# Joint products for half blocks of maxima, six weight chunks decoded later, and three smaller moves in a fused attention and two-layer network

## The chip, the core and the metric

The kernel runs on one core of a Trainium2 chip. The core has five engines with a queue of instructions each, which run in order and wait for each other by semaphores: PE (TensorE, matrix products), DVE (VectorE), ACT (ScalarE), POOL (GpSimd) and SP (SyncE, which here issues nearly all DMA transfers). The metric is the device time of one execution in microseconds (us), lower is better.

## What is computed

```python
q_pool = q.reshape(B, H, S // 2, 2, D).mean(axis=3)      # B, H, S, D = 4, 8, 1152, 64
scores = matmul(q_pool, k.transpose(0, 1, 3, 2)) / sqrt(D)
attn = exp(scores - max(scores)); attn = attn / (sum(attn) + 1e-9)
x = matmul(attn, v)                # heads side by side: 2304 tokens x 512
h = x @ moe_w_in;  x = (h * cos(h)) @ moe_w_out          # 512 -> 2048 -> 512
h = x @ moe2_w_in; out = where(h > 0, h, exp(min(h, 0)) - 1) @ moe2_w_out
```

The weights come as 64-bit floats, everything else as 32-bit floats.

## The kernel before

PE multiplies in a fast 32-bit form (fp32r) that keeps fewer bits, so operands are split into a high and a low part and a product becomes two or three products that add up in PSUM. The 64-bit weights are decoded on the chip from their raw words: `decode_tasks` (L84 to L130) gives ten tasks for one half (w_in or w_out) of one of the 16 chunks of a layer: a fetch of 512 KB (`raw`, two buffers), five DVE instructions, an ACT copy to the high part, one more DVE instruction, and two (`far`, L128 and L129) that make the low part, on POOL for the first layer and on DVE for the second. Their work tiles `m` and `e` have two buffers in the attention and one in the MLP (`dec2`, L655).

**Attention.** The 32 heads are worked on in 16 pairs. A pair takes 36 steps, 18 a head (two halves of 288 pooled queries by nine chunks of 128 keys). A step has two products for scores (`ps`, L453 and L455, of which the second takes the row maxima off), an exponential on ACT (`e`, L458), for five chunks of nine a split of `e` into `eh` and `el` (ACT L466, POOL L467), and seven steps later the products with v into `acc` (L482 to L486). Between these the next pair is prepared by a plan of step numbers (L574 to L621): keys and queries are transposed on PE (L340), copied as high parts (L349, L353), low parts are taken (L357, L364), and DMAs place them (L329). The maxima come from `unit` (L394): products of a block of 128 queries with 384 keys into `pm` (L400) and a reduction by DVE (L407). A head has 4.5 blocks of queries, so the fifth block of a pair holds half a block of each head, and its `unit` has two products that add up, each with zeros where the other head's queries stand. Sums of squares (`square`, ACT, L314; five a pair) go to `judge`, whose result `fits` says at the end whether a second, exact network has to run. `weight_work` decodes the first layer's weights meanwhile, paced by step counts (L635); four chunks stay in SBUF, twelve go to DRAM (`w_d`, L150) and are fetched again by `fetch_w` (L154).

The first pair is prepared before the steps begin (L537 to L562): all transposes of both heads, their high and low parts, v, three blocks of maxima of the first head, the sums of squares.

**MLP.** `mlp` runs two layers of six blocks of 384 tokens, each block 16 steps, one chunk of 128 hidden units a step. Step i issues `h_step(i)` (12 products, L673 to L675, then ACT L682 and DVE L683), `g_step(i-1)` (ACT L696 and L697, DVE L699, ACT L704, POOL L705, which make `gh` and `gl`) and `o_step(i-3)` (12 products into `po`, L729; nine wider ones in the second layer). `split_x` (L190) makes the next block's tokens ready in steps 8 to 11: a product with the reciprocal sums (DVE L194, first layer only), the high part (ACT L197), the low part (DVE L198). From the second block on `weight_work(1, ...)` decodes the second layer's weights, four or five tasks a step. `ps_h` has four buffers, so PE can be three steps ahead of `g_step`.

## Time and profile before

| | |
|---|---|
| time, median of 3 runs (lowest to highest) | 1386.76 us (1385.75 to 1387.06) |
| time of the profiled execution | 1385.99 us |
| its span | 1384.2 us |
| PE busy | 1349.6 us, 98% of the span |
| DVE, ACT, POOL busy | 822.8, 819.8, 700.5 us (59%, 59%, 51%) |
| DMA | 177 MB moved, q1 takes 44.9% of 16 engines' span |

The span runs from the first to the last instruction of the program. Products are pipelined: their durations overlap, and what a product takes of PE's time is the distance from its start to the next one's. The table's PE time is the union of overlapping durations. The attention ends and the MLP begins at 567.7 us; the first layer ends at about 970.5 us.

### The profile page before, as it was taken

The page shows a single profiled execution, that of the slowest core. Times are in us where ns is not written, and L with a number is a line of the kernel's source. Part 1 is how long each engine was busy: PE and PEld are TensorE (multiplying, and loading weights), DVE is VectorE, ACT ScalarE, POOL GpSimd, SP SyncE. Part 2 cuts the span into 40 slices and gives each one's busy share as a digit, 9 for nine tenths or more (in the row PEclk, how much of TensorE's full clock was granted, in tenths as well). Part 3 has the DMA queues.
Part 4 walks back from the last instruction along what each step waited for, and adds up shares of the span by engine and source line. Part 5 has one row for each costly group of instructions (what it writes and reads, how often), then busy time and mean ns, then how long its engine had stood idle before and what let it go on. Part 6 is the DMA issues. An engine that isn't in the chain of part 4 may idle for free.

```text
span 1384.2 us, 22762 instructions
## 1 busy us (share of the span) xinstructions
PE 1349.6 (98%) x7683; PEld 1235.9 (89%) x7683; DVE 822.8 (59%) x1454; ACT 819.8 (59%) x2080; POOL 700.5 (51%) x823
## 2 busy tenths in 40 slices
PE   6999999999999999999999999999999999999998
PEld 5888888888888888899999999999999999999997
DVE  5678897887888878236887888788121212111111
ACT  5778878878888787655554555455533433343332
POOL 5668888787888888322232223232333333333332
PEclk9999999999999999999999999999999999999999
DMA  4566667787768775572352535269501010101000
GB/s 97 132 144 148 159 137 188 173 203 179 186 174 198 181 191 137 185 274 96 117 168 93 176 107 189 71 207 364 211 1 47 0 46 1 46 1 46 1 24 26
DMA packets 164543, 177.25 MB, mean 128 GB/s; under 512 B 83872, under 2 KB 135840, under 8 KB 164416
## 3 DMA queue, kind: packets, MB, share of 16 engines
q1 hardware_dynamic: 164416, 175.70, 44.9%
q8 instruction: 63, 1.03, 0.3%
q14 instruction: 64, 0.52, 0.1%
HBM read 105.46 MB, written 43.66 MB: 108 GB/s over the span
## 4 chain that ended last, share of the span: by engine, by line
PE 66%; issue 17%; DVE 8%; POOL 7%; ACT 1%; DMA 0%; POOLq 0%; SPq 0%; DVEq 0%; ACTq 0%
PE po L729 18%; PE acc L486 7%; POOL gl L705 6%; PE ph L675 6%; PE ph L673 6%; PE ph L674 6%; PE pm L400 5%; PE ps L453 5%; PE ps L455 4%; DVE mm L407 3%; PE acc L484 2%; PE acc L482 2%; PE acc L483 2%; PE pk L340 1%; DVE m L117 1%
## 5 line engine op out<-in xcount | busy, mean ns | idle before, releaser
L705 POOL TENSOR_TENSOR gl<-u,gh 128x384 fp32r<-128x384 f32 x192 | 207.6, 1081 | 328.8 <-ACT gh L704 322.5
L467 POOL TENSOR_TENSOR el<-e,eh 128x288 fp32r<-128x288 f32 x320 | 271.8, 857 | 115.7 <-ACT eh L466 83.9
L458 ACT ACTIVATE e<-ps 128x288 f32<-128x288 f32 x576 | 234.4, 413 | 110.1 <-PE ps L455 84.0
L675 PE MATMUL ph<-xh,w 128*128 128x384 f32 x768 | 257.9, 336 | 0.0
L673 PE MATMUL ph<-xh,w 128*128 128x384 f32 x768 | 257.7, 336 | 0.0
L674 PE MATMUL ph<-xl,w 128*128 128x384 f32 x768 | 257.4, 335 | 0.0
L407 DVE TENSOR_REDUCE mm<-pm 128x1 f32<-128x384 f32 x432 | 222.9, 549 | 53.7 <-PE pm L400 52.1
L729 PE MATMUL po<-gh,w 128*128 128x384 f32 x768 | 211.4, 336 | 0.4 <-ACT gh L704 0.4
L453 PE MATMUL ps<-qst,kst 128*128 128x288 f32 x576 | 201.3, 349 | 2.5 <-ACT e L458 2.4
L702 DVE SCALAR_TENSOR_TENSOR u<-ph,a 128x384 f32<-128x384 f32 x96 | 52.8, 554 | 225.7 <-POOL a L688 225.7
L729 PE MATMUL po<-w,gh 128*128 128x512 f32 x576 | 179.6, 393 | 0.0
L400 PE MATMUL pm<-kst,qst 128*128 128x384 f32 x480 | 168.8, 405 | 7.7 <-DVE mm L407 6.1
L686 ACT ACTIVATE a<-ph 128x384 f32<-128x384 f32 x96 | 47.2, 492 | 214.2 <-PE ph L675 210.8
L455 PE MATMUL ps<-q,k 69*128 69x288 f32 x576 | 171.9, 298 | 0.9 <-DVE q L429 0.8
L486 PE MATMUL acc<-e,vt 128*66 128x288 f32 x512 | 166.0, 405 | 0.0
L704 ACT CAST gh<-u 128x384 fp32r<-128x384 f32 x192 | 97.5, 508 | 113.7 <-DVE u L699 88.6
L688 POOL TENSOR_SCALAR a<-a 128x384 f32<-128x384 f32 x96 | 50.3, 524 | 223.6 <-ACT a L687 214.6
L673 PEld LDWEIGHTS ph<-xh,w 128*128 128x128 f32 x768 | 144.3, 188 | 4.1
L674 PEld LDWEIGHTS ph<-xl,w 128*128 128x128 f32 x768 | 144.2, 188 | 3.9
L675 PEld LDWEIGHTS ph<-xh,w 128*128 128x128 f32 x768 | 144.2, 188 | 0.0
L729 PEld LDWEIGHTS po<-gh,w 128*128 128x128 f32 x768 | 140.1, 188 | 1.4 <-ACT gh L704 1.0
L466 ACT CAST eh<-e 128x288 fp32r<-128x288 f32 x320 | 137.0, 428 | 0.0
(87 smaller groups left out, 2548.6 us busy)
## 6 DMA issues: line engine op xcount, KB each, us to landing
w_d<-wd SPq DMA_DIRECT2D x56, 512.0 KB
w<-w_d SPq DMA_DIRECT2D x56, 512.0 KB
raw<-in_moe_w_in_dram SPq DMA_DIRECT2D x32, 512.0 KB
raw<-in_moe_w_out_dram SPq DMA_DIRECT2D x32, 512.0 KB
vt<-in_v_dram SPq DMA_DIRECT2D x32, 288.0 KB
kr<-in_k_dram SPq DMA_DIRECT2D x30, 288.0 KB
k<-uk SPq DMA_DIRECT2D x30, 288.0 KB
qr<-in_q_dram SPq DMA_DIRECT2D x32, 256.0 KB
```

What stands on the lines that cost most here:

```text
L400: nc.tensor.matmul(ps[:, 0:W], qst[:, i * P:(i + 1) * P], kst[:, u * W:(u + 1) * W], start=first, stop=last and not exact)
L407: nc.vector.reduce_max(mm[:, x, u:u + 1], ps[:, 0:W], axis=AX.X)
L453: nc.tensor.matmul(ps[:, 0:HALF], kst[:, c * P:(c + 1) * P], qst[:, qs], start=True, stop=False)
L455: nc.tensor.matmul(ps[:, 0:HALF], k2[0:KR, c * P:(c + 1) * P], q2[0:KR, qs], start=False, stop=True)
L458: nc.scalar.activation(e, ps[:, 0:HALF], AF.Exp, scale=SCALE)
L467: nc.gpsimd.tensor_tensor(el, e, eh.bitcast(F32), ALU.subtract)
L486: nc.tensor.matmul(acc[0:VW, 0:HALF], vt[:, j * NC + c, :], *e, start=first, stop=last)
L673: nc.tensor.matmul(h, wh, xh, start=(c == 0), stop=False)
L674: nc.tensor.matmul(h, wh, xl, start=False, stop=False)
L675: nc.tensor.matmul(h, wl, xh, start=False, stop=(c == KD - 1))
L705: nc.gpsimd.tensor_tensor(gl, u, gh.bitcast(F32), ALU.subtract)
L729: nc.tensor.matmul(o, a, b_, start=st and t == 0, stop=sp and t == 2)
```

## The change

Five things are changed.

1. From the second pair on, the fifth block's `unit` makes one product where it made two: `qd`, a new tile that holds the half blocks of both heads in its two diagonal quarters (copied there by POOL, two copies of 64 x 64 a pair), by the high part of both heads' keys (`uk`). The limit in `judge` is halved.
2. The w_out halves of chunks 4, 6, 8, 10, 12 and 14 of the first layer (`LATE`) are decoded no more during the attention, stored and fetched, but by `late_work` in the first block of the MLP, five tasks a step from step 0 on, straight into the weight tile.
3. The sums of squares of a pair are three instructions, not five: keys in two pieces, all queries in one.
4. The first pair is prepared head by head: queries are loaded from ACT's queue and added on DVE; the first head's transposes, high parts and three blocks of maxima go first (with the high parts of 64 rows alone), then the second head's, for which the transposes are made a second time. The splits of v for the next pair stand at steps 27 and 31 instead of both at 27.
5. In the first layer, from the third block of tokens on, `split_x` runs its two DVE instructions on POOL.

```diff
@@ network
+    LATE = range(NPREW, KF, 2)
@@ weight_work
             for half in range(2):
+                if half and layer == 0 and f in LATE:
+                    continue
...
+    def late_work(dec_p):
+        rest = []
+        for f in LATE:
+            first, *others = decode_tasks(0, f, 1, wt[0, f][:, 1], dec_p)
+            yield first
+            yield from rest
+            rest = others
+        yield from rest
@@ fetch_w
-        for half in range(2):
+        for half in range(1 if layer == 0 and f in LATE else 2):
@@ split_x
+        eng = nc.vector if layer or blk < 2 else nc.gpsimd
         if layer == 0:
-            nc.vector.tensor_tensor(src, src, rb[:, c, :], ALU.mult)
+            eng.tensor_tensor(src, src, rb[:, c, :], ALU.mult)
...
-        nc.vector.tensor_tensor(lo, src, hi.bitcast(F32), ALU.subtract)
+        eng.tensor_tensor(lo, src, hi.bitcast(F32), ALU.subtract)
@@ load
+            queue = nc.sync if n else nc.scalar
             for j in range(2):
-                nc.sync.dma_start(
+                queue.dma_start(
...
-            for c in range(0, NC, step):
-                for j in range(2):
+            for j, c in itertools.product(range(2), range(0, NC, step)):
@@ prep_tasks
-            nfull, tail, third = SQ // P, SQ % P, NC // 3
-            pieces = [(kr[:, third * i:third * (i + 1)], P, i) for i in range(3)] + [(qp[:, 0:nfull], P, 3)]
-            if tail:
-                pieces.append((qp[0:tail, nfull:], tail, 4))
+            nfull, tail = SQ // P, SQ % P
+            pieces = [(kr[:, 0:NC // 2], 0), (kr[:, NC // 2:], 1), (qp, 3)]
...
-                nc.gpsimd.tensor_tensor(
-                    qp[0:m, i0:i1], qr[0:m, i0:i1, :, 0], qr[0:m, i0:i1, :, 1], ALU.add)
+                (nc.gpsimd if n else nc.vector).tensor_tensor(
+                    qp[0:m, i0:i1, js], qr[0:m, i0:i1, js, 0], qr[0:m, i0:i1, js, 1], ALU.add)
...
+                        if n and tag == "q" and blocks[0] == (0 if j else NQB - 2):
+                            src = qst[j][0:D, j * OFF:P] if j else qst[j][0:D, (NQB - 1) * P:SQ]
+                            nc.gpsimd.tensor_scalar(
+                                qd[j * D:(j + 1) * D, j * OFF:j * OFF + SQ % P], src.bitcast(F32),
+                                1.0, 0.0, ALU.mult, ALU.add)
@@ unit
+                if len(parts) == 2 and n and not exact:
+                    nc.tensor.matmul(ps[:, 0:W], qd, highs[n][:, u * W:(u + 1) * W],
+                                     start=True, stop=True)
+                    parts = []
+                kr = slice(0, D) if pool is ps_s and not exact else slice(0, P)
...
-                        ps[:, 0:W], qst[:, i * P:(i + 1) * P], kst[:, u * W:(u + 1) * W],
+                        ps[:, 0:W], qst[kr, i * P:(i + 1) * P], kst[kr, u * W:(u + 1) * W],
@@ judge
-                    fits, both[:, 0:1], (LIMIT * 2.0 ** 12) ** 2 * D, None, ALU.is_le)
+                    fits, both[:, 0:1], (LIMIT * 2.0 ** 11) ** 2 * D, None, ALU.is_le)
@@ attention, before the pairs
+        adds[0]()
+        q_groups[0][0](ps_a, "a", slice(0, 1))
+        for g in k_groups:
+            g[0](heads=slice(0, 1))
+        first = [q_groups[0]] + k_groups
+        for _, high, _ in first:
+            high((0,))
...
+        for t in units(0, HB, ps_s, "s"):
+            t()
...
+        combine(0, 0, HB)
+        spread(0, 0, HB, ps_s, "s")
...
+        for t in adds[1:]:
+            t()
...
+        for put, high, low in q_groups[1:]:
             put(ps_a, "a")
...
+        for put, high, low in first:
+            put(*((ps_a, "a") if low is first[0][2] else ()))
+            high((1,))
+            low((1,))
         split_v(0)
@@ attention, the pairs
-        n_ww = 2 * KF * 10 + (KF - NPREW)
+        n_ww = (2 * KF - len(LATE)) * 10 + (2 * (KF - NPREW) - len(LATE))
...
-                at(SV, lambda: split_v(n + 1))
+                for j in range(2):
+                    at(SV + 4 * j, lambda j=j: split_v(n + 1, (j,)))
@@ mlp
+        late = late_work(dec_p)
...
                 fetch_w(0, NPREW + 4 + i, wp2)
+            if i < KF:
+                run_some(late, 5)
```

PE, pair 1's preparation in the steps of pair 0. First before, then now: `pm_4` is the half-block product, `ps` and `acc` are the steps of the running pair.

```order
L484 MATMUL acc_1_536<-el_17_548,vh_132 66x288
L400 MATMUL pm_3_0_645<-kst_0_279,qst_130 128x384
L400 MATMUL pm_4_0_648<-kst_0_279,qst_130 128x384
L400 MATMUL pm_4_0_648<-kst_1_280,qst_131 128x384
L453 MATMUL ps_7_652<-qst_129,kst_1_166 128x288
L455 MATMUL ps_7_652<-q_1_168,k_1_125 128x288
```

```order
L515 MATMUL acc_1_553<-el_17_565,vh_132 66x288
L431 MATMUL pm_3_0_659<-kst_0_295,qst_130 128x384
L423 MATMUL pm_4_0_662<-uk_293,qd 128x384
L484 MATMUL ps_7_665<-qst_129,kst_1_160 128x288
L486 MATMUL ps_7_665<-q_1_162,k_1_125 128x288
```

The two rows of `pm_4` have become one; three such places a pair.

SP's queue as the MLP begins. In front of both pieces stand the fetches of `w_4` to `w_7`, eight halves before and six now. First before: the scale rows `rb` of the next block, then the weights; the brackets name the semaphores waited for, where DMAHW0 to DMAHW7 are taken in turn, one by each transfer.

```order
L180 DMA rb_9141<-rec_d 64x4x192 [waits DMAHW5_49]
L180 DMA rb_9141<-rec_d 64x4x192 [waits DMAHW6_49]
L180 DMA rb_9141<-rec_d 64x4x192 [waits DMAHW7_49]
L180 DMA rb_9141<-rec_d 64x4x192 [waits DMAHW0_49]
L157 DMA w_8_9163<-w_d 128x1024 [waits DMAHW1_49]
L157 DMA w_8_9163<-w_d 128x1024 [waits DMAHW2_49]
L157 DMA w_9_9190<-w_d 128x1024 [waits DMAHW3_49]
L157 DMA w_9_9190<-w_d 128x1024 [waits DMAHW4_49]
L210 DMA rec_d<-sm_9101 128x36 [waits DMAHW5_49,DVE_49]
L157 DMA w_10_9220<-w_d 128x1024 [waits DMAHW6_49]
L157 DMA w_10_9220<-w_d 128x1024 [waits DMAHW7_49]
L157 DMA w_11_9263<-w_d 128x1024 [waits DMAHW0_49]
```

```order
L183 DMA xin_1_8974<-x_d 128x4x384 [waits DVE_49]
L193 DMA rb_8976<-rec_d 64x4x192 [waits DMAHW7_49]
L193 DMA rb_8976<-rec_d 64x4x192 [waits DMAHW0_49]
L193 DMA rb_8976<-rec_d 64x4x192 [waits DMAHW1_49]
L193 DMA rb_8976<-rec_d 64x4x192 [waits DMAHW2_49]
L170 DMA w_8_8998<-w_d 128x1024 [waits DMAHW3_49]
L110 DMA raw_4_1_9000<-in_moe_w_out_dram 128x1024 [waits DMAHW4_49]
L110 DMA raw_6_1_9004<-in_moe_w_out_dram 128x1024 [waits DMAHW5_49]
L170 DMA w_9_9035<-w_d 128x1024 [waits DMAHW6_49]
L170 DMA w_9_9035<-w_d 128x1024 [waits DMAHW7_49]
```

The raw words of chunks 4 and 6 now stand behind the fetches of chunks 4 to 8 and the tokens and scales of the next block.

DVE's queue at the same place, from the MLP's first instruction: `u_0_i` is step i's tile of `h_step` (L683, now L739) and of `g_step` (L699, now L755). First before, then now.

```order
L683 SCALAR_TENSOR_TENSOR u_0_1_9180<-a_0_1_9179,ph_0_1_9166 128x384 [waits Activation_49]
L699 SCALAR_TENSOR_TENSOR u_0_0_9160<-a_0_0_9159,ph_0_0_9146 128x384 [waits DVE_49,Activation_49]
L683 SCALAR_TENSOR_TENSOR u_0_2_9207<-a_0_2_9206,ph_0_2_9193 128x384 [waits Activation_49,Pool_49]
L699 SCALAR_TENSOR_TENSOR u_0_1_9180<-a_0_1_9179,ph_0_1_9166 128x384 [waits Activation_49]
L208 TENSOR_SCALAR sm_9101<-sm_9101 128x36 [waits DMAHW3_49]
```

```order
L739 SCALAR_TENSOR_TENSOR u_0_0_8995<-a_0_0_8994,ph_0_0_8981 128x384 [waits DMAHW5_49,DMAHW2_49,Activation_49]
L119 TENSOR_SCALAR m_4_1_9001<-raw_4_1_9000 128x512 [waits DMAHW4_49]
L120 TENSOR_SCALAR m_4_1_9001<-m_4_1_9001 128x512 [waits DVE_49]
L121 TENSOR_SCALAR m_4_1_9001<-m_4_1_9001 128x512 [waits DVE_49]
L739 SCALAR_TENSOR_TENSOR u_0_1_9025<-a_0_1_9024,ph_0_1_9011 128x384 [waits Activation_49]
L755 SCALAR_TENSOR_TENSOR u_0_0_8995<-a_0_0_8994,ph_0_0_8981 128x384 [waits Activation_49]
L123 SCALAR_TENSOR_TENSOR m_4_1_9001<-raw_4_1_9000,m_4_1_9001 128x512 [waits DVE_49]
L126 TENSOR_SCALAR e_4_1_9002<-m_4_1_9001 128x512 [waits DVE_49]
L128 SCALAR_TENSOR_TENSOR e_4_1_9002<-raw_4_1_9000,e_4_1_9002 128x512 [waits DVE_49]
L739 SCALAR_TENSOR_TENSOR u_0_2_9057<-a_0_2_9056,ph_0_2_9043 128x384 [waits Activation_49,Pool_49]
L755 SCALAR_TENSOR_TENSOR u_0_1_9025<-a_0_1_9024,ph_0_1_9011 128x384 [waits Activation_49]
```

The first instruction of the decode, which waits for the transfer's semaphore DMAHW4, stands ahead of step 1's and step 0's.

DVE in steps 8 and 9 of that block, where the second block's tokens are split (`xin`, `xl`). First before, then now.

```order
L683 SCALAR_TENSOR_TENSOR u_0_8_9436<-a_0_8_9435,ph_0_8_9422 128x384 [waits Activation_49,Pool_49]
L194 TENSOR_TENSOR xin_1_9139<-xin_1_9139,rb_9141 128x384 [waits DMAHW6_49,DMAHW5_49,DMAHW7_49,DMAHW4_49,DMAHW0_49]
L198 TENSOR_TENSOR xl_1_0_9441<-xin_1_9139,xh_1_0_9440 128x384 [waits PE_49,Activation_49]
L699 SCALAR_TENSOR_TENSOR u_0_7_9397<-a_0_7_9396,ph_0_7_9383 128x384 [waits Activation_49]
L683 SCALAR_TENSOR_TENSOR u_0_9_9477<-a_0_9_9476,ph_0_9_9463 128x384 [waits Activation_49,Pool_49]
```

```order
L739 SCALAR_TENSOR_TENSOR u_0_8_9322<-a_0_8_9321,ph_0_8_9308 128x384 [waits Activation_49,Pool_49]
L208 TENSOR_TENSOR xin_1_8974<-xin_1_8974,rb_8976 128x384 [waits DMAHW7_49,DMAHW1_49,DMAHW0_49]
L212 TENSOR_TENSOR xl_1_0_9327<-xin_1_8974,xh_1_0_9326 128x384 [waits PE_49,Activation_49]
L755 SCALAR_TENSOR_TENSOR u_0_7_9278<-a_0_7_9277,ph_0_7_9264 128x384 [waits Activation_49]
L119 TENSOR_SCALAR m_12_1_9258<-raw_12_1_9257 128x512 [waits DMAHW2_49,Pool_49]
L120 TENSOR_SCALAR m_12_1_9258<-m_12_1_9258 128x512 [waits DVE_49]
L121 TENSOR_SCALAR m_12_1_9258<-m_12_1_9258 128x512 [waits DVE_49]
L739 SCALAR_TENSOR_TENSOR u_0_9_9371<-a_0_9_9370,ph_0_9_9357 128x384 [waits Activation_49]
```

The decode of chunk 12 stands between the steps, and its first instruction waits for a transfer and for POOL, whose last instruction on chunk 10 still reads `m`.

## Rows read from the trace of the kernel before

**Rows 1.** Stretches: length, busy time (x instructions) by engine, granted clock, DMA share, GB/s.

```profile
28.00:567.70 539.70, 528.63 (x3307) 459.89 (x3308) 433.11 (x793) 430.97 (x1269) 429.81 (x501) 1.00 0.67 164
...
629.30:903.80 274.50, 269.77 (x1538) 266.64 (x1537) 228.77 (x373) 146.02 (x304) 73.83 (x64) 1.00 0.41 131
```

**Rows 2.** Timeline, PE: start us, duration us, line, product; MLP begins.

```profile
567.71 0.34 PE L673 MATMUL ph<-xh,w 128*128 128x384 f32 x1
...
567.88 0.33 PE L674 MATMUL ph<-xl,w 128*128 128x384 f32 x1
```

**Rows 3.** Timeline, ACT: ends of half heads, pairs 1 and 3.

```profile
63.94 0.40 ACT L490 COPY xo<-acc 65x288 f32<-65x288 f32 x1
...
81.65 0.40 ACT L490 COPY xo<-acc 65x288 f32<-65x288 f32 x1
...
134.37 0.40 ACT L490 COPY xo<-acc 65x288 f32<-65x288 f32 x1
...
151.03 0.40 ACT L490 COPY xo<-acc 65x288 f32<-65x288 f32 x1
```

**Rows 4.** Groups, 64 to 555 us: shapes xcount | busy us, mean ns | idle before.

```profile
L117 DVE TENSOR_SCALAR m<-raw 128x512 uint32<-128x512 uint32 x32 | 29.9, 935 | 0.7 <-DMA raw<-in_moe_w_in_dram 0.7
...
L128 POOL TENSOR_TENSOR m<-m,wd 128x512 f32<-128x512 f32 x24 | 31.6, 1316 | 0.1
...
L314 ACT ACTIVATE junk<-kr 128x384 f32<-128x384 f32 x42 | 22.2, 528 | 0.0
...
L365 POOL TENSOR_SCALAR qst<-qst 64x192 fp32r<-64x192 f32 x28 | 11.6, 430 | 1.2
```

**Rows 5.** Timeline of the start: first maxima on DVE, first exponential on ACT.

```profile
14.65 4.29 DVE L407 TENSOR_REDUCE mm<-pm 128x1 f32<-128x384 f32 x9
...
20.93 0.41 ACT L458 ACTIVATE e<-ps 128x288 f32<-128x288 f32 x1 [4.14 <-PE ps L455]
```

**Rows 6.** Timeline, MLP steps 0 to 3: DVE, PE, and SP, the DMA queue.

```profile
570.57 0.56 DVE L683 SCALAR_TENSOR_TENSOR u<-a,ph 128x384 f32<-128x384 int32 x1 [14.14 <-ACT a L682]
...
571.04 3.81 SPq L157 DMA_DIRECT2D w<-w_d  x8
...
574.99 0.55 DVE L699 SCALAR_TENSOR_TENSOR u<-a,ph 128x384 f32<-128x384 f32 x1 [1.84 <-ACT a L697]
...
576.14 0.44 PE L729 MATMUL po<-gh,w 128*128 128x384 f32 x1
...
591.15 0.58 SPq L157 DMA_DIRECT2D w<-w_d  x1
```

**Rows 7.** Groups by shape, 640 to 900 us, DVE, then POOL.

```profile
L699 DVE SCALAR_TENSOR_TENSOR u<-a,ph 128x384 f32<-128x384 f32 x60 | 33.0, 550 | 12.0 <-ACT a L697 12.0
...
L126 DVE SCALAR_TENSOR_TENSOR e<-raw,e 128x512 f32<-128x512 uint32 x24 | 21.4, 892 | 0.4
...
L121 DVE SCALAR_TENSOR_TENSOR m<-raw,m 128x512 uint32<-128x512 uint32 x24 | 20.8, 868 | 0.6
...
L119 DVE TENSOR_SCALAR m<-m 128x512 uint32<-128x512 uint32 x25 | 20.0, 800 | 0.7
...
L124 DVE TENSOR_SCALAR e<-m 128x512 uint32<-128x512 uint32 x24 | 14.4, 600 | 0.7
...
L117 DVE TENSOR_SCALAR m<-raw 128x512 uint32<-128x512 uint32 x25 | 14.0, 561 | 0.3
...
L118 DVE TENSOR_SCALAR m<-m 128x512 f32<-128x512 f32 x25 | 12.0, 481 | 0.7
...
L705 POOL TENSOR_TENSOR gl<-u,gh 128x384 fp32r<-128x384 f32 x60 | 70.1, 1168 | 190.9 <-ACT gh L704 187.0 <-PE po L729 2.2 <-PE ph L675 1.7
```

**Rows 8.** Timeline, PE: first product of MLP blocks 1, 5 and 6.

```profile
629.26 0.34 PE L673 MATMUL ph<-xh,w 128*128 128x384 f32 x1
...
903.79 0.34 PE L673 MATMUL ph<-xh,w 128*128 128x384 f32 x1
...
970.53 0.34 PE L673 MATMUL ph<-xh,w 128*128 128x384 f32 x1
```

More of the change, by code (lines that the diff above doesn't have):

```diff
@@ L261, in load @@
                 if SQ % P:
-                    nc.sync.dma_start(
+                    queue.dma_start(
                         out=qr[0:SQ % P, nfull, j].rearrange("p r d -> p (r d)"),
@@ L281, in load_v, with split_v @@
                 )
-        def split_v(n):
-            for j in range(2):
+        def split_v(n, heads=(0, 1)):
+            for j in heads:
                 src = vts[n % 2][:, j * NC + SPLIT[0]:(j + 1) * NC:2, 0:D]
@@ L334, in group, with put @@
                 ps = {}
-                def put(pool=ps_big, t="big"):
+                def put(pool=ps_big, t="big", heads=slice(0, 2)):
                     ps[0] = pool.tile([P, 512], F32, tag=t, name=f"p{tag}{n}_{blocks[0]}")
@@ L350, in high, with low @@
                         return
-                    for j in range(2):
+                    for j in heads:
                         dst = kst[j][0:D, cols] if tag == "k" else qst[j][0:D, j * OFF + c0:j * OFF + c0 + w]
                         nc.scalar.copy(dst, ps[0][j * D:(j + 1) * D, 0:w])
-                def low():
+                def low(heads=(0, 1)):
                     if n and tag == "k":
@@ L358, in low @@
                         return
-                    for j in range(2):
+                    for j in heads:
                         qc = slice(j * OFF + c0, j * OFF + c0 + w)
@@ L379, in prep_tasks @@
                 adds.append(lambda: add_q(nfull, NQB))
+            if n == 0:
+                adds = [
+                    lambda: add_q(0, 3, slice(0, 1)), lambda: add_q(0, 3, slice(1, 2)),
+                    lambda: add_q(3, nfull), *adds[1:]]
             q_groups = [
@@ L540, in attention @@
         units, combine, spread = max_tasks(0)
-        for t in adds:
-            t()
-        for put, _, _ in q_groups:
+        HB = (HALF + P - 1) // P
+        assert HB <= 3
+        adds[0]()
[5 more added lines that the diff above has]
+            high((0,))
+        if exact:
+            for _, _, low in first:
+                low((0,))
+        for t in units(0, HB, ps_s, "s"):
+            t()
+        if not exact:
+            for _, _, low in first[:2]:
+                low((0,))
+        combine(0, 0, HB)
+        spread(0, 0, HB, ps_s, "s")
+        if not exact:
+            for _, _, low in first[2:]:
+                low((0,))
+        for t in adds[1:]:
+            t()
+        minus_ones(1)
+        for t in vhs:
+            nc.gpsimd.memset(t[:, :, D:VW].bitcast(F32), 1.0)
+        for x, t in enumerate(qsts):
+            z = t[:, 0:OFF] if x % 2 else t[:, SQ:]
+            nc.gpsimd.memset(z.bitcast(F32), 0.0)
+        for put, high, low in q_groups[1:]:
             put(ps_a, "a")
-        for _, high, low in q_groups:
             high()
             low()
-        for put, high, low in k_groups:
-            put()
-            high()
-            low()
+        for put, high, low in first:
+            put(*((ps_a, "a") if low is first[0][2] else ()))
+            high((1,))
+            low((1,))
         split_v(0)
-        HB = (HALF + P - 1) // P
-        for t in units(0, HB, ps_s, "s"):
-            t()
-        combine(0, 0, HB)
-        spread(0, 0, HB, ps_s, "s")
+        for i in range(2, 4):
+            minus_ones(i)
         if not exact:
```

32 lines of the change are left out of this document (17 added, 15 removed).

## The prediction

> **What bounds the kernel now.** I read three things in order. First the stretches [rows 1]: in the attention (28 to 567.7 us) PE is busy 529 of 540 us and DVE, ACT and POOL 430 to 433 us each, four fifths; in blocks 1 to 4 of the MLP PE is busy 270 of 274.5 us and DVE 229. So PE sets the end in both stages and what counts is what PE waits for. Second, the spacing of products, because durations overlap: two products of 384 columns start 0.17 us apart though each lasts 0.34 [rows 2]. An MLP step has 24 of them, and block 5 takes 970.53 - 903.79 = 66.74 us [rows 8], 4.17 us a step, 0.174 us a product. Third, where PE falls behind: blocks 1 to 4 take 903.79 - 629.26 = 274.5 us for 4 x 66.74 = 267.0, so 7.5 us are lost there [rows 8]; their DVE carries the decode, two instructions a step of 0.55 us, and the splits [rows 7]. The start costs 20.9 us to the first exponential [rows 5]. And the first MLP steps have a lag I will need: step 0's second DVE instruction starts at 574.99 us, and the first product that needs it, `po`, at 576.14 [rows 6].
>
> All sums are made against the profiled execution, 1385.99 us, which is 0.77 us under the median of the runs; the forecast adds the 0.77 again.
>
> **The half-block product.** 15 pairs lose 3 products each, 45 x 0.174 = 7.8 us of PE [rows 8]. The reductions that read them stay. PE is the bound around them, so I take -7.8; if DVE's reductions were what PE waited for there, it would be 0. POOL gains 30 copies of 64 columns, each under the 0.43 us of the 192-column copy [rows 4], under 13 us, while it loses the 12 decode instructions of part two at 1.32 us [rows 4], 15.8 us: no net load.
>
> **Decode moved out of the attention, fewer squares.** DVE loses 6 x 6 decode instructions of up to 0.94 us [rows 4], at most 34 us of its 433; ACT loses two squares a pair, each at most 0.53 us [rows 4], at most 16 us of its 431. How much of that reaches PE? Pair 1 has no decode before its step 24 and pair 3 has it throughout. The same two half heads (18 steps) take 81.65 - 63.94 = 17.7 us in pair 1 and 151.03 - 134.37 = 16.7 us in pair 3 [rows 3]; pair 1 has there five more maxima products, 0.9 us. The rest, 0.1 us, says that the decode costs PE next to nothing. For the squares and the divided split of v I can only bound: 0 to -9 us, about half of all they take off ACT. I take -4.
>
> **The first pair.** The first maxima are reduced from 14.65 us on and the first exponential starts at 20.93 [rows 5]. POOL's memsets and the second head no longer stand ahead of the maxima, so these can start some 6 us sooner. But the second head's copies, twelve repeated transposes, the splits of v and the squares all stay ahead of the first exponential in ACT's queue, and they now begin only after the first head's maxima (4.29 us) and lows. What is won in front is queued again behind. I take 0, from -3 to +3 us.
>
> **Late decode, the wait for data.** Here I expect the loss. DVE runs in order, and the decode of chunk 4 stands between step 0's first instruction (570.57 us before [rows 6]) and its second. It waits for `raw_4`. SP can begin to fetch only at 571.04 [rows 6], when the attention's buffers are free. Ahead of `raw_4` and including it go eight halves of 512 KB, the next block's tokens and its scales. Before the change exactly these bytes (eight halves, tokens, scales) ended with the last `rb`, whose semaphore DMAHW0 is the one that `w_11` waits for, and `w_11` was issued at 591.15 us [rows 6]. So `raw_4` lands at about 591.15. Then come three decode instructions, 0.56 + 0.48 + 0.80 = 1.84 us, and step 1's, 0.55 [rows 7]; step 0's second starts at 593.6 instead of 574.99. PE can run three steps ahead and has done all of that by 576.14, so it stands still for the difference: +18.6 us. Bounds: 0, if the data came in time, to 21, if POOL's and ACT's first instructions are slow as well.
>
> **Late decode, the chain afterwards.** `m` and `e` have one buffer in the MLP and the last readers of a chunk are on POOL. From one chunk's first DVE instruction to the next one's the chain is: three instructions 1.84, two of a step 1.10, three more 0.87 + 0.60 + 0.89 = 2.36, two of the next step 1.10, the copy `gh` 0.60 (576.14 - 574.99 - 0.55), `gl` 1.17, and POOL's second decode instruction, like its first 1.32 us [rows 4, 6, 7]. Sum 9.5 us for two steps, for which PE needs 8.34. Since the stall has used up PE's lead, each of the five handovers costs 1.15 us, +5.7. In steps 8 to 11 the next block's split lies in the same DVE queue, two instructions of 0.55 with an ACT copy of about 0.6 between them, 1.7 us a step, +6.8. Together +12.5; bounds 0 (all hidden by PE's lead) to 14.
>
> **PE's clock.** The granted clock reads 1.00 in both stretches [rows 1], and nothing in them shows PE idle for 18 us in mid-kernel. If products run at half speed for the 24 after the gap, that is 4.2 us, if not, 0; part of it lies under the chain. I take +1.
>
> **Splits on POOL.** In blocks 1 to 4 DVE loses 16 x 2 instructions of 0.55 us in the steps just before the lost 7.5 us, while POOL was busy 74 of 274.5 us [rows 1]. I take -7, bounds 0 to -7.5. DVE's decode gets slower beside a busy POOL: L117 takes 0.94 us in the attention, where POOL is busy four fifths, and 0.56 in the MLP [rows 4, 7]; that eats part of the gain, not all, since DVE still loses 1.1 us a step. The Trainium skill ("SBUF — State Buffer", section "Who interferes with whom") is harsher: DVE and GpSimd share one pair of ports, an instruction of either that needs it holds it to its end, and the other blocks fully. By that rule the splits could cost more than they save; it is the third rival.
>
> **Sum.** -7.8 - 4 + 0 + 18.6 + 12.5 + 1 - 7 = +13.3: 1399.3 us for a profiled execution, 1400 with the 0.77. Since some of the chain may hide in ACT's waits, I say 1399.
>
> **Rivals.**
> First, the data comes in time, because transfers overtake or DVE is later than I think: the 18.6 and the 1 fall away, 1379 us. For it: the scales are small rows and could be passed. Against it: rows of one queue, and the byte count. This one ends faster. Second, the chain hides: the stall stands, but the 12.5 vanish because ACT and POOL run ahead between, 1387 us, no change. For it: POOL has idle time, 74 of 274.5 us busy in the blocks after [rows 1]; against it: every link waits for the one before. Third, the ports: each split puts two POOL instructions of 1.17 us [rows 7] where DVE had two of 0.55; if DVE stands still for all of them its load grows by 1.24 us a split, and 16 splits cost 20 us instead of saving 7: 1426 us. It decides as soon as DVE, now 229 of 274.5 us, no longer fits into its steps. Against it: in the attention DVE does its work next to a POOL that is busy four fifths. That the exact network has to run after the halved limit I leave out: the inputs are normal with a spread of 0.8, so that sums of 64 to some hundreds of their squares are in the hundreds and their product under a million, and the limit is (2^11)^2 x 64 = 270 million.
>
> **How the numbers follow.** Forecast 0.76 (own range 1389 to 1410: attention gain 4 to 17, chain 6 to 14, clock up to 4, splits 0 to -7.5), data in time 0.11, chain hidden 0.08, ports 0.05. The range 1381 to 1412 holds the forecast's and the second rival's cases and the upper part of the first's. About 0.2%, 2.8 us, is what a measurement of this kernel can tell from no change. Faster: nearly all of the first rival and the low end of the second, 0.13; same: most of the second and the forecast's lowest edge, 0.08; slower 0.79.
>
> **What would show it.** In the profile after: DVE idle some 20 us in front of the first late decode instruction, released by the DMA `raw<-in_moe_w_out`; PE idle about 18 us between block 0's step 3 and its first `po`; in the steps after, DVE waiting for POOL at the first decode instruction of each chunk, and steps of 4.7 us, 6 and more in 8 to 11; blocks 1 to 4 at 67 us each; a pair of the attention 0.5 to 1 us shorter; the first exponential near 21 us. If DVE's wait for `raw` is under 5 us, the sum falls by its largest term, and the sign with it.

## The result and the profile after

The changed kernel takes 1406.54 us, median of 4 runs (1405.38 to 1407.92), against 1386.84 us: a ratio of 1.0144, 95% interval [1.0126, 1.0162]. It is slower by 19.7 us. Its profiled execution took 1405.38 us with a span of 1403.2, 19.0 above the span of before.

The first product of each MLP block tells in which stage that is. Timeline of PE, changed kernel: start, duration, engine, line, product; blocks 0, 1, 5 and 6.

```profile
559.71 0.34 PE L729 MATMUL ph<-xh,w 128*128 128x384 f32 x1
...
652.68 0.34 PE L729 MATMUL ph<-xh,w 128*128 128x384 f32 x1
...
919.85 0.34 PE L729 MATMUL ph<-xh,w 128*128 128x384 f32 x1
...
986.60 0.34 PE L729 MATMUL ph<-xh,w 128*128 128x384 f32 x1
```

Beside the kernel before ([rows 2, 8]) this reads: the attention ends 559.71 - 567.71 = 8.0 us earlier. Block 0 takes 92.97 us where it took 61.55, 31.4 more. Blocks 1 to 4 take 267.17 where they took 274.53, 7.4 less. Block 5 is the same. Sum +16.1; the missing 2.9 us lie behind PE's last product, which starts at 1393.65 us (9.6 before the span ends) where it started at 1377.59 (6.6 before its end).

Block 0 on DVE. Timeline of the changed kernel; in brackets the idle time ahead and what ended it.

```profile
562.51 0.55 DVE L739 SCALAR_TENSOR_TENSOR u<-a,ph 128x384 f32<-128x384 int32 x1 [14.08 <-ACT a L738]
582.74 0.43 DVE L119 TENSOR_SCALAR m<-raw 128x512 uint32<-128x512 uint32 x1 [19.68 <-DMA raw<-in_moe_w_out_dram]
...
584.47 0.55 DVE L755 SCALAR_TENSOR_TENSOR u<-a,ph 128x384 f32<-128x384 f32 x1
...
591.50 0.43 DVE L119 TENSOR_SCALAR m<-raw 128x512 uint32<-128x512 uint32 x1 [2.25 <-POOL w L131]
...
600.26 0.43 DVE L119 TENSOR_SCALAR m<-raw 128x512 uint32<-128x512 uint32 x1 [2.91 <-POOL w L131]
...
608.93 0.43 DVE L119 TENSOR_SCALAR m<-raw 128x512 uint32<-128x512 uint32 x1 [2.98 <-POOL w L131]
...
613.62 0.54 DVE L739 SCALAR_TENSOR_TENSOR u<-a,ph 128x384 f32<-128x384 int32 x1
614.08 1.18 DVE L208 TENSOR_TENSOR xin<-xin,rb 128x384 f32<-128x384 f32 x1
615.84 0.56 DVE L212 TENSOR_TENSOR xl<-xin,xh 128x384 fp32r<-128x384 f32 x1 [0.58 <-ACT xh L211]
616.82 0.55 DVE L755 SCALAR_TENSOR_TENSOR u<-a,ph 128x384 f32<-128x384 f32 x1 [0.42 <-ACT a L753]
620.32 0.43 DVE L119 TENSOR_SCALAR m<-raw 128x512 uint32<-128x512 uint32 x1 [2.94 <-POOL w L131]
...
633.82 0.43 DVE L119 TENSOR_SCALAR m<-raw 128x512 uint32<-128x512 uint32 x1 [2.97 <-POOL w L131]
```

The second line is the wait for data, 19.68 us, ended by the transfer `raw`. Behind it stands step 0's second instruction (L755), 24.8 us after the block's start where it was 7.3 ([rows 2, 6]: 574.99 - 567.71): 17.5 us late. Then every chunk's first instruction (L119) waits 2.3 to 3.0 us for POOL's last instruction on the chunk ahead. The chunks start 8.76, 8.76 and 8.67 us apart without a split between them, 11.39 with one, 13.50 with two. PE does not feel all of that: by the starts of its steps, steps 4 to 8 take 4.16 to 4.19 us as before, and steps 9 to 13 take 4.39, 5.89, 9.05, 4.46 and 9.72 us, 12.7 more than before.

PE, same kernel: the last product ahead of the gap, the first behind it, and the first of the next step.

```profile
567.86 0.34 PE L731 MATMUL ph<-xh,w 128*128 128x384 f32 x1
585.62 0.69 PE L785 MATMUL po<-gh,w 128*128 128x384 f32 x1 [17.42 <-ACT gh L760]
...
589.94 0.35 PE L729 MATMUL ph<-xh,w 128*128 128x384 f32 x1
```

Stretches around it, all engines: length, busy time (x instructions) of PE, PEld, DVE, ACT, POOL, then granted clock, DMA share, GB/s.

```profile
566.00:584.00 18.00, 2.19 (x13) 1.87 (x11) 1.19 (x3) 0.93 (x2) 0.00 (x0) 0.68 1.04 354
584.00:588.00 4.00, 1.99 (x5) 1.59 (x6) 3.93 (x7) 2.46 (x5) 1.85 (x2) 0.50 0.29 115
588.00:592.00 4.00, 4.00 (x21) 4.00 (x20) 1.68 (x6) 1.84 (x4) 3.06 (x3) 0.83 0.26 39
...
652.70:919.90 267.20, 267.20 (x1538) 266.92 (x1537) 222.48 (x342) 146.83 (x304) 108.98 (x96) 1.00 0.43 134
```

After 17.4 us without a product PE is granted 0.50, the lower of its levels, and from its first `po` to the next step it needs 4.32 us (3.10 before, 576.14 to 579.24). The step of the gap took 23.99 us where it had taken 5.29: 18.7 more, 17.5 of them the late start and 1.2 the slow products. In the last row PE is busy all of 267.20 us: the splits are off its path.

### The profile page after: what moved, and what is told of

Same layout as the page of the kernel before. It is cut to its first block, busy times and chain, and to the rows that moved or that the text cites. A ratio compares the mean times of both kernels' runs of the same rounds, so it can differ in the third digit from the quotient of the medians.

```text
span 1403.2 us, 22604 instructions
## 1 busy us (share of the span) xinstructions
PE 1347.7 (96%) x7650; PEld 1233.2 (88%) x7650; DVE 804.0 (57%) x1427; ACT 817.8 (58%) x2016; POOL 739.8 (53%) x884
## 4 chain that ended last, share of the span: by engine, by line
PE 84%; DVE 6%; DMA 3%; ACT 3%; POOL 2%; issue 2%; SPq 0%; POOLq 0%; ACTq 0%; DVEq 0%
PE po L785 28%; PE ph L731 9%; PE ph L729 9%; PE ph L730 9%; PE acc L517 6%; PE ps L484 5%; PE ps L486 4%; PE pm L431 4%; DVE mm L438 3%; PE acc L515 2%; PE acc L513 2%; PE acc L514 2%; PE pk L355 1%; ACT e L489 1%; POOL el L498 1%
## 5 line engine op out<-in xcount | busy, mean ns | idle before, releaser
L498 POOL TENSOR_TENSOR el<-e,eh 128x288 fp32r<-128x288 f32 x320 | 267.5, 842 | 105.0 <-ACT eh L497 67.8
L785 PE MATMUL po<-gh,w 128*128 128x384 f32 x768 | 214.7, 340 | 23.0 <-ACT gh L760 23.0
L431 PE MATMUL pm<-kst,qst 128*128 128x384 f32 (+1 forms) x390 | 144.1, 410 | 4.1 <-DVE mm L438 1.7
```

The lines of the kernel that those rows point to most:

```text
L431: nc.tensor.matmul(ps[:, 0:W], qst[kr, i * P:(i + 1) * P], kst[kr, u * W:(u + 1) * W], start=first, stop=last and not exact)
L498: nc.gpsimd.tensor_tensor(el, e, eh.bitcast(F32), ALU.subtract)
L785: nc.tensor.matmul(o, a, b_, start=st and t == 0, stop=sp and t == 2)
```

## The experiments

All are stage lengths of one profile each (MLP begins; block 0; blocks 1 to 4), and the median of the timed runs with its ratio to the kernel before, timed beside it. Where the attention's code is the same but for two fetches in its last pair (changed kernel, e3, e4, r11) the MLP begins within 2.8 us. When pair 1 begins they are already 2.4 us apart (55.3 to 57.7 us, last section), and from there on they repeat to 2.1 us. A difference of this size between two profiles says nothing by itself.

| kernel | MLP begins | block 0 | blocks 1 to 4 | time us | ratio [95%] |
|---|---|---|---|---|---|
| before | 567.7 | 61.5 | 274.5 | 1386.8 | |
| changed | 559.7 | 93.0 | 267.2 | 1406.5 | 1.0144 [1.0126, 1.0162] |
| e1 no late decode | 572.4 | 61.5 | 267.2 | 1383.2 | 0.9973 [0.9964, 0.9983] |
| e2 late decode alone | 559.4 | 93.4 | 274.2 | 1411.9 | 1.0172 [1.0155, 1.0189] |
| e3 raw words early | 561.7 | 77.6 | 267.2 | 1392.4 | 1.0042 [1.0028, 1.0056] |
| e4 and low parts on DVE | 562.5 | 74.3 | 267.1 | 1386.9 | 0.9999 [0.9990, 1.0009] |
| n1 e1, five squares | 575.4 | 61.6 | 267.2 | 1387.0 | 1.0003 [0.9994, 1.0013] |
| n2 e1, copies on DVE | 568.4 | 61.6 | 267.1 | 1380.1 | 0.9952 [0.9938, 0.9966] |
| n3 e1, v split at 27 | 571.9 | 61.6 | 267.1 | 1383.9 | 0.9983 [0.9972, 0.9995] |
| n4 joint product alone | 569.5 | 61.5 | 274.6 | 1389.5 | 1.0026 [1.0015, 1.0037] |
| r9 e1, copies by DMA | 591.5 | 61.5 | 267.1 | 1403.0 | 1.0121 [1.0105, 1.0136] |
| r10 late decode ordered | 577.0 | 65.7 | 267.4 | 1392.0 | 1.0033 [1.0019, 1.0048] |
| r11 block 1's splits on POOL | 561.5 | 94.6 | 267.2 | 1408.2 | 1.0148 [1.0133, 1.0164] |
| r12 r10, copies on DVE | 557.5 | 65.5 | 267.1 | 1375.2 | 0.9928 [0.9915, 0.9940] |

**Without the late decode (e1).** In the changed kernel:

```diff
-    LATE = range(NPREW, KF, 2)
+    LATE = range(0)
```

> The changed kernel without the late decode: all twelve stored chunks are decoded during the attention again and fetched whole; the joint product, the three squares, the first pair head by head and the splits on POOL stay. My theory: the late decode is the whole loss and gave the attention little. Then block 0 of the MLP takes its old 61.5 us (93.0 in the changed kernel), blocks 1 to 4 keep 267, and the MLP begins at 559.7 to 562 us, since six chunks of decode more on DVE cost PE at most 2 us: 1370 to 1374 us. Rival: the relief of DVE is what shortened the attention; then the MLP begins at 564 or later and the time is 1375 or more.

First products of blocks 0 and 1:

```profile
572.45 0.34 PE L729 MATMUL ph<-xh,w 128*128 128x384 f32 x1
...
633.99 0.34 PE L729 MATMUL ph<-xh,w 128*128 128x384 f32 x1
```

Block 0 is back at 61.5 us and blocks 1 to 4 keep 267.2. But the MLP begins at 572.4, 12.7 us later than in the changed kernel and 4.7 later than before. The rival holds: the relief is what shortened the attention, and the other parts together made it longer.

**The late decode alone (e2)**, in the kernel before: `LATE`, `late_work`, the shorter `fetch_w`, the line in the MLP's loop, and the number of tasks by which the decode in the attention is paced (`n_ww`).

> The kernel before with the late decode alone. My theory: block 0 takes 93 us for 61.5, the attention ends at 566 to 567.7, blocks 1 to 4 keep their 274.5: 1415 to 1418 us. Rival, the relief is worth something: the attention ends at 564 or before, 1413 or less. Rival, the loss in block 0 comes from the late decode together with the other parts: block 0 then takes clearly less than 93.

93.4 us in block 0: the loss belongs to this part alone. The attention ends 8.3 us earlier by it, and the time, 1411.85, is just under the 1413 us of the second theory. So six half chunks of decode cost the attention 8.3 us in the kernel before and 12.7 in the changed one. In the 8.3 there is one thing more: `n_ww` counted 332 of 344 tasks in the kernel before, which left twelve for the time behind the last step, and it counts all 278 here. The last pair, where these would show, is 0.7 us shorter (31.15 and 30.49 us).

**Raw words early (e3).** In the changed kernel, in the last pair:

```diff
+                for f in LATE[:2]:
+                    at(6, lambda f=f: early.update({(0, f, 1): fetch_raw(0, f, 1)}))
...
```

> The changed kernel with one thing moved: the raw words of chunks 4 and 6 are fetched in the last pair of the attention, where both buffers of raw are free, and not behind the fetches of the MLP. My theory of two separate terms: DVE's wait of 19.7 us for the first raw words and the 18.7 us that PE lost by it go away. The second term, 12.7 us in steps 9 to 13 by the chain through POOL and by the splits, stays in part, since PE now enters it with a lead of up to three steps (12.5 us): block 0 takes 62 to 74 us, the time is 1376 to 1388. Rival, the second term is a consequence of the late start (everything is pushed into the splits): it vanishes altogether, block 0 takes 62, 1376. Rival, the chain is slower by itself than PE and the lead hides nothing: block 0 takes 74 or more.

The 18.7 us at step 3 are gone (5.30 us, as before the change), and block 0 falls by 15.4 to 77.6: still more than my theory's 74. The third theory has the number right, but for another reason as well: there is a second wait for data, chunk 8's. DVE, this kernel:

```profile
588.33 0.43 DVE L131 TENSOR_SCALAR m<-raw 128x512 uint32<-128x512 uint32 x1 [6.42 <-DMA raw<-in_moe_w_out_dram]
```

It costs 5.0 us at step 7 (9.18 for 4.18). Steps 11 to 13 lose 9.4 of the other 11.0 us, so the lead of three steps does not hide the chain.

**Low parts on DVE as well (e4).**

```diff
-        far = nc.vector if layer else nc.gpsimd
+        far = nc.vector if layer or (half and f in LATE) else nc.gpsimd
```

> As the run before, and the two instructions that make the low part of a late chunk are on DVE, not on POOL: DVE no longer waits for POOL to give m back, and POOL has gl alone. DVE's work rises to about 6.5 us per two steps, for which PE needs 8.34. If the handover to POOL is what is slow: block 0 at 62 to 65 us, 1376 to 1379, and better than the run before. If the splits are what is slow (product, ACT's copy, low part in one queue with the decode): the steps 9 to 12 still exceed 4.2 us, and it gains nothing on the run before or loses.

In block 0 this is 3.3 us better than e3, but far from 62 to 65. 5.3 us still go to chunk 8's data in step 7, and steps 11 to 14 still exceed 4.2 us. The handover through POOL looks like the smaller part; this run does not show it apart from that wait and from DVE's two instructions more a chunk.

**The joint product alone (n4)**, in the kernel before: `qd`, its two POOL copies, the single product, the limit.

> The kernel before with the joint product alone, its copies on POOL. My sum: 45 products of 0.174 us less, the attention ends at 567.7 - 7.8 = 560 us, 1378 to 1379 us in all. Theory Q: the copies on POOL, which still has the decode here, give most of it back: 564 or later. Theory S: the sum holds, as the squares are the old ones.

My sum falls. The products are gone, and steps 17, 21 and 25 of a pair are 0.16 to 0.17 us shorter each (means over pairs 2 to 14), but steps 14, 16 and 29 are 0.21, 0.22 and 0.14 us longer, and the attention ends 1.8 us later than before. That is less than two profiles can tell, but the timed runs say it too: 3.0 us slower than the kernel before beside them (1386.52). PE's own idle time in pairs 2 to 14 grows from 7.8 us (of 443.4) to 13.6 (of 446.8). ACT shows one wait that grew. Groups from 64 to 555 us, the exponentials: count, busy us, mean ns, then idle time by what ended it; before, then this kernel.

```profile
L458 ACT ACTIVATE e<-ps 128x288 f32<-128x288 f32 x519 | 211.0, 413 | 93.3 <-PE ps L455 68.0 <-POOL el L467 10.2 <-PE pm L400 4.5
```

```profile
L473 ACT ACTIVATE e<-ps 128x288 f32<-128x288 f32 x516 | 209.8, 413 | 95.8 <-PE ps L470 61.9 <-POOL el L482 23.4 <-POOL qp L329 2.7
```

POOL's copies, same kernel and stretch:

```profile
L373 POOL TENSOR_SCALAR qd<-qst 64x64 fp32r<-64x64 f32 x28 | 11.1, 397 | 0.9
```

The exponentials wait 13.2 us longer for POOL's `el`, and 11.1 us of copies stand in POOL's queue. The next run tests whether the one comes from the other.

**The copies on DVE (n2), the squares (n1), the split of v (n3)**, each in e1:

```diff
-                            nc.gpsimd.tensor_scalar(
+                            nc.vector.tensor_scalar(
                                 qd[j * D:(j + 1) * D, j * OFF:j * OFF + SQ % P], src.bitcast(F32),
```

> Same base; the two copies a pair into the diagonal tile are made by DVE, not by POOL. Theory Q: the MLP begins 4 us or more earlier than 572.4, and the waits of the exponentials for POOL's el fall. Theory S: no difference beyond 1.5 us; if DVE is the tighter engine there, later.

The MLP begins 4.1 us earlier, and the exponentials' wait for `el` falls from 26.4 us to 16.4 (the groups from 64 to 555 us):

```profile
L489 ACT ACTIVATE e<-ps 128x288 f32<-128x288 f32 x512 | 209.2, 414 | 99.6 <-PE ps L486 60.5 <-POOL el L498 26.4 <-PE acc L515 1.8
```

```profile
L489 ACT ACTIVATE e<-ps 128x288 f32<-128x288 f32 x517 | 211.2, 414 | 94.3 <-PE ps L486 66.9 <-POOL el L498 16.4 <-POOL qp L340 1.0
```

Theory Q holds, by just its bound: the copies on POOL cost 10.0 us of these waits and some 4 us of the attention (3.1 by time). But with the copies off POOL the attention, with the other parts of e1 in it, still ends no earlier than in the kernel before (568.4 and 567.7), so they are not the whole reason why the 7.8 us do not come. In n1 the five old instructions stand in place of the three larger ones:

```diff
...
-            pieces = [(kr[:, 0:NC // 2], 0), (kr[:, NC // 2:], 1), (qp, 3)]
...
+            pieces = [(kr[:, third * i:third * (i + 1)], P, i) for i in range(3)] + [(qp[:, 0:nfull], P, 3)]
+            if tail:
+                pieces.append((qp[0:tail, nfull:], tail, 4))
```

> Base: the changed kernel without the late decode, whose MLP begins at 572.4 us, 4.7 later than in the kernel before although 45 products are gone. Here the five smaller sums of squares are put back in place of the three larger ones. Theory S, the larger squares are what costs: they hold ACT up to 0.75 us each and delay the exponential; the MLP begins at 566 us or earlier. Theory Q, the two copies into the diagonal tile on POOL (0.57 to 0.66 us each) push the low parts of the exponentials back, on which ACT waits: it stays within 1.5 us of 572.4.

Theory S falls: 3.8 us slower by time, 2.9 by the start of the MLP. In the profiles all but 0.4 of that arises before pair 1 (it begins at 57.9 us, in e1 at 55.3), for which the last section has the clock; from pair 1 on three squares or five make no difference that two profiles can tell. In n3 both splits of v stand at one step again:

```diff
-                for j in range(2):
-                    at(SV + 4 * j, lambda j=j: split_v(n + 1, (j,)))
+                at(SV, lambda: split_v(n + 1))
```

> Same base; both splits of v stand at step 27 again, not at 27 and 31. Steps 29, 30 and 33 of a pair took 0.1 to 0.2 us longer after the change. If the later second split does that, the MLP begins 2 to 4 us earlier than 572.4; if it is the rest of the queue, within 1.5 us of it.

The MLP begins 0.5 us earlier: the divided split of v makes no difference that can be told.

**The copies by DMA (r9)**, in e1:

```diff
-                            nc.gpsimd.tensor_scalar(
-                                qd[j * D:(j + 1) * D, j * OFF:j * OFF + SQ % P], src.bitcast(F32),
-                                1.0, 0.0, ALU.mult, ALU.add)
+                            place(qd[j * D:(j + 1) * D, j * OFF:j * OFF + SQ % P], src)
```

> Base: the changed kernel without the late decode. The diagonal tile is filled by two DMA transfers a pair from SP's queue, so that neither POOL nor DVE has a copy more. Theory Q: POOL's copies are what ate the joint product's 7.8 us. Then the exponentials' waits for el fall from 26 us to some 10 as in the kernel before, and the MLP begins 8 us before 572.4 or more: 560 to 564, 1372 to 1376 us in all. Rival: PE is ahead of ACT's and POOL's chain in any case, and what it saves in steps 17 to 25 it waits again in steps 14, 16 and 29; then it begins at 568 or later, as with the copies on DVE (568.4), 1380 or more.

Later than the rival's bound, but not for its reason: the MLP begins 19 us later than in e1. The waits from 64 to 560 us (who, for what: us, times, longest):

```profile
PEld pm L421 <- issue: 12.3, 4, 4.4
...
PE pm L421 <- DMA qd<-qst: 11.8, 5, 4.0
```

The joint product (L421) now waits up to 4 us for its operand. "issue" has no releaser in the trace; each of these four weight loads starts 0.03 us ahead of a product that waits for `qd`, so both rows are one wait of some 12 us. Of the 19 us, 2.9 are there when pair 1 begins (58.2 and 55.3 us), some 4 are not accounted for. The exponentials' wait for `el` fell as with the copies on DVE (16.2 us), but what the joint product is worth without a copy on any engine this run cannot tell, as PE waits for the transfers instead.

**Block 1's splits on POOL (r11)**, in the changed kernel:

```diff
-        eng = nc.vector if layer or blk < 2 else nc.gpsimd
+        eng = nc.vector if layer or blk < 1 else nc.gpsimd
```

> The changed kernel with one thing more: the splits of block 1's tokens, in steps 8 to 11 of block 0, are on POOL too. If the splits in DVE's queue are what makes steps 9 to 13 12.7 us too long (each puts 2.6 us between the two instructions of a step: product, ACT's copy, low part, ACT's sine behind it), these steps fall to 3 us or less, block 0 to 83 or 84 us, 1396 in all. Rival: the handover through POOL is the limit; POOL has two instructions of about 1 us more a step, each ahead of the decode's, and the steps stay as long or get longer.

The rival: 94.6 us, no gain. POOL, then DVE, in step 8:

```profile
615.29 1.74 POOL L130 TENSOR_TENSOR m<-m,w 128x512 f32<-128x512 f32 x1
616.98 1.02 POOL L208 TENSOR_TENSOR xin<-xin,rb 128x384 f32<-128x384 f32 x1
618.62 1.02 POOL L212 TENSOR_TENSOR xl<-xin,xh 128x384 fp32r<-128x384 f32 x1 [0.62 <-ACT xh L211]
```

```profile
619.56 0.55 DVE L755 SCALAR_TENSOR_TENSOR u<-a,ph 128x384 f32<-128x384 f32 x1 [3.21 <-ACT a L753]
```

DVE waits 3.21 us for ACT's square behind the sine (L753), since ACT's copy `xh` stands ahead of the sine in ACT's queue and waits for the split's multiplication (L208), which now stands behind the decode on POOL. The split moved to the other engine of the same chain.

**The late decode ordered (r10)**: e4, block 1's splits on POOL, the copies by DMA, the weight tiles of chunks 4 to 15 taken before their fetches, and in the MLP's loop

```diff
-            if f == (5 if i >= KF else 0) and nxt[0] < 2:
+            if f == (5 if i >= KF else 3) and nxt[0] < 2:
...
-            if NPREW + 4 + i < KF:
-                fetch_w(0, NPREW + 4 + i, wp2)
+            if i >= 3 and NPREW + 1 + i < KF:
+                fetch_w(0, NPREW + 1 + i, wp2)
```

> The changed kernel with the late decode arranged by what the runs showed: raw words of chunks 4 and 6 fetched in the last pair, later raw words ahead of the weights that are needed after them (chunks 8 to 15 are fetched five steps ahead, not eight, and the next block's tokens from step 3 on), low parts of late chunks on DVE, block 1's splits on POOL, and the diagonal tile filled by DMA. My theory: block 0's loss is made of three waits, for data, for the handover through POOL, and for the splits in DVE's queue, and nothing else is behind them: block 0 takes 61.5 to 64 us (93.0 in the changed kernel), and with the attention at 552 to 556 the time is 1364 to 1370 us. Rival: DVE or ACT is too full for the decode in any order: 70 us or more in block 0.

Block 0 takes 65.7 us: with the raw words in front, POOL out of the decode and DVE rid of the splits 27 of the 31 us are gone, a little less than I expected. The run takes these steps together and does not give the share of each. The attention has r9's wait again (577.0).

**And the copies on DVE (r12).**

```diff
-                            place(qd[j * D:(j + 1) * D, j * OFF:j * OFF + SQ % P], src)
+                            nc.vector.tensor_scalar(
+                                qd[j * D:(j + 1) * D, j * OFF:j * OFF + SQ % P], src.bitcast(F32),
+                                1.0, 0.0, ALU.mult, ALU.add)
```

> The ordered late decode of the run before last, with the diagonal tile's copies on DVE in place of the DMA. DVE has room in the attention now that six chunks of decode are gone from it, and on POOL the copies cost waits. If the terms add: the attention ends 4 us before the changed kernel's 559.7, at 555 to 558 us, block 0 takes 65 to 67 us, blocks 1 to 4 267: 1370 to 1375 us, below the kernel before. If the copies on DVE only move the wait (maxima late instead of el), the attention ends at 560 or later, 1376 or more.

1375.24 us (1374.0 to 1378.6), 0.9928 of the kernel before: faster than the kernel before and the changed one, and its stages are what was expected, with the time at the upper edge. First products of blocks 0, 1 and 5:

```profile
557.51 0.34 PE L743 MATMUL ph<-xh,w 128*128 128x384 f32 x1
...
622.99 0.34 PE L743 MATMUL ph<-xh,w 128*128 128x384 f32 x1
...
890.13 0.34 PE L743 MATMUL ph<-xh,w 128*128 128x384 f32 x1
```

In this kernel the exponentials wait 9.6 us for `el` from 64 to 555 us, no longer than before the change (10.2):

```profile
L501 ACT ACTIVATE e<-ps 128x288 f32<-128x288 f32 x533 | 217.6, 415 | 89.2 <-PE ps L498 65.6 <-POOL el L510 9.6 <-POOL qp L352 2.9
```

The attention ends 1.8 us earlier than in e2 (559.4), which has the same relief and still two products for the half blocks; the squares and the split of v, by which the two differ as well, made no difference in n1 and n3. So most of the joint product's 7.8 us are not there even with the copies on DVE. Part of it PE waits again: in pairs 2 to 14 it is idle for 7.5 us here and for 4.1 in e2.

## Why the prediction was right, and where it was not

The forecast was 1399 in 1381 to 1412, slower by 12; measured were 1406.5, slower by 19.7. The sign and the main cause held: a wait for data and a chain of handovers in block 0. Of the difference between the sum, +13.3, and the spans, +19.0, 3.8 us lie in the attention and 2.9 behind the last product; block 0 and blocks 1 to 4 came 0.7 and 0.4 us below their terms. By its own steps:

- **Wait for data, +18.6.** Right. The idle time of DVE is 19.68 us, and the raw words came 23.0 us after the MLP's first product, where the bytes ahead in the queue had said 591.15 - 567.71 = 23.4. The late start is worth 17.5. e3 took this wait away, and its 18.7 us with it.
- **Clock, +1.** Right: 1.2 us at granted clock 0.50.
- **Chain through POOL and the splits, +12.5.** The sum was right (steps 9 to 13 lose 12.7 us), its two terms were not, and that these nearly make up for each other is luck. The chain takes 8.7 us for two steps and not 9.5, so that a handover costs 0.4 and not 1.15. "The stall has used up PE's lead" failed as well: steps 4 to 8, with the first handovers in them, lose nothing. A split costs 2.7 us alone and 4.8 for two (11.39 - 8.7, 13.50 - 8.7) and not 1.7: I had left out ACT's sine and square, which stand behind the split's copy in ACT's queue (0.42 us more of waiting), and a multiplication (L208) of 1.18 us beside a busy POOL (0.55 without). That both lie in one chain, r11 showed: the split moved to POOL gains nothing.
- **Splits on POOL in blocks 1 to 4, -7.** Right: -7.4, in every kernel that has this part and in none that has not. The rival of the ports falls for these blocks.
- **The half-block product, -7.8.** Wrong. Alone it gains nothing: 1.8 us later by the attention's end, 3.0 us slower by time (n4). What failed is "PE is the bound around them" and "no net load" on POOL: I had added up POOL's busy time over the whole attention, where it has room, and not looked at its queue in the steps where the copies stand. There they push `el` back and ACT's exponentials wait for it; moving them to DVE gives some 4 us back (n2). Why the rest of the 7.8 does not come is open: PE takes in steps 14, 16 and 29 what it saves in 17, 21 and 25. The bound "0 if PE waits there for DVE" had the size, but named neither POOL nor these steps.
- **Decode and squares in the attention, -4.** Wrong too, to the other side: the decode alone is worth -8.3 (e2), in company -12.7 (e1). The step that failed is the comparison of pairs 1 and 3 in [rows 3]: those stretches end about step 25, while e2 gains in steps 16, 29, 33 and 34 (0.15, 0.20, 0.09 and 0.08 us a pair, means over pairs 2 to 14), over half of it behind them; and what it gains within them, some 0.24 us a pair, the comparison had as 0.1. The squares, once past the start, made 0.4 us in n1, too little to tell.
- Together I had -11.8 for the attention and it became -8.0. That this is as near as it is is luck: two wrong terms that partly cancel.
- **First pair, 0.** Right in the sum, within its bounds of 3 us: pair 1 begins at 55.3 us and began at 56.0, and in e3, with the same first pair, at 57.7 (last section). The first exponential, expected near 21 us, comes at 23.54, later than before (20.93, [rows 5]): the second head's copies, the splits of v and the squares stand ahead of it in ACT's queue, as the prediction said; that this costs the first exponential 2.6 us it did not say.
- Not foreseen: the 2.9 us behind the last product.

Open: e1's attention is 4.7 us longer than before, of which the joint product explains 1.8. From pair 1 on e1 is still 2.5 us behind n4, and neither the squares (n1) nor the split of v (n3), put back one at a time, gives it back. Part of it may be spread between profiles (2.1 us where the code is the same). One difference that no run takes by itself is the decode's pace, which the diff of the change shows: with all chunks in the attention `n_ww` counts 344 tasks in e1 and 332 in n4, so e1 decodes 3.6% faster. The stretch behind the last product was between 6.6 and 9.8 us in all these kernels; I have made no experiment on it.

## What to carry to other kernels

Before work is moved to the start of a stage, count the bytes that stand ahead of its data in the queue: here that gave the landing to 0.4 us, and the raw words, fetched one stage earlier into buffers that were free (e3), took the wait away and cost the attention nothing that two profiles can tell. Room on an engine is to be sought in the steps where the new instruction stands, not in its busy share: 11 us of copies on a POOL busy for four fifths cost some 4 us of the attention here (n2). And products taken off the busiest engine need not shorten a stage: 45 of them, 7.8 us, gained nothing in n4. Where a chain runs through several engines, moving a link to another engine of that chain need not help: r11 gained nothing by it.

## What the runs showed of the hardware that I had not expected

**DVE and POOL side by side.** The decode's L126 took 0.43 us in some chunks and three times as long in others. DVE, then POOL, in the changed kernel:

```profile
585.66 1.27 DVE L126 TENSOR_SCALAR e<-m 128x512 uint32<-128x512 uint32 x1
...
603.18 0.43 DVE L126 TENSOR_SCALAR e<-m 128x512 uint32<-128x512 uint32 x1
603.64 1.39 DVE L128 SCALAR_TENSOR_TENSOR e<-raw,e 128x512 f32<-128x512 uint32 x1
```

```profile
585.64 1.00 POOL L761 TENSOR_TENSOR gl<-u,gh 128x384 fp32r<-128x384 f32 x1 [27.46 <-ACT gh L760]
...
603.22 1.26 POOL L761 TENSOR_TENSOR gl<-u,gh 128x384 fp32r<-128x384 f32 x1 [2.99 <-ACT gh L760]
604.44 1.74 POOL L130 TENSOR_TENSOR m<-m,w 128x512 f32<-128x512 f32 x1
```

The long L126 lies beside POOL's `gl` and ends 0.29 us after it. The long L128 (0.69 elsewhere) lies across two POOL instructions: it starts while `gl` runs and ends 0.55 us after it, and POOL's L130, which starts meanwhile, takes 1.74 us and about 1.28 in the attention. The Trainium skill ("SBUF — State Buffer", section "Who interferes with whom") says that these two engines share ports under an exclusive lock; these rows agree with it. It is 0.7 to 0.8 us for such an instruction in the chain of block 0; blocks 1 to 4, with POOL busier than before, show no loss by it.

**The clock at the start.** In the kernels with the new first pair PE stands still for 1.0 to 2.4 us until about 24 us, waiting for ACT's first exponential. Stretches of PE, 24 to 26 us, in the changed kernel and in n1: length, busy (x products), granted clock, DMA share, GB/s.

```profile
24.00:26.00 2.00, 2.00 (x12) 1.00 0.93 212
```

```profile
24.00:26.00 2.00, 1.40 (x5) 0.50 0.75 171
```

What the grant is behind this gap differs from profile to profile, also where the first pair's instructions are the same (changed kernel, e3, e4, r11), and the start of pair 1 goes with it. At 1.00 in all of 24 to 30 us (changed kernel, e1, n2, n3, r12) pair 1 begins at 55.2 to 55.6 us, at 0.50 in part of it (e4, r10, r11) at 56.3 to 57.1, at 0.50 in all of it (n1, e3, r9) at 57.7 to 58.2. Between the changed kernel and e3 this is worth 2.4 us.

The old first pair is not free of such a spread. Products of one step at that time, in the kernel before and in n4:

```profile
24.37 0.44 PE L453 MATMUL ps<-qst,kst 128*128 128x288 f32 x1
24.61 0.44 PE L455 MATMUL ps<-q,k 69*128 69x288 f32 x1
```

```profile
24.35 0.30 PE L468 MATMUL ps<-qst,kst 128*128 128x288 f32 x1
24.48 0.30 PE L470 MATMUL ps<-q,k 69*128 69x288 f32 x1
```

They start 0.24 us apart in the kernel before, as they do at 0.50 in n1 (25.89 and 26.13), and 0.13 in n4; pair 1 begins at 56.0 and 54.9 us. The stretch of the kernel before reads 1.00 there all the same, so at the start of a profile the spacing of the products has to be read beside the granted clock.
